# Strassen's seven half-size products for the second MoE product, on a TensorE-bound kernel

## The chip, the cores and the metric

The kernel runs on one core of a Trainium2 chip. The metric is the device time of that core in microseconds (us). Four executions before the change took 411.81, 412.22, 412.71 and 460.8 us. The last is over 1.5% above the fastest and counts as a slow one; everything below uses the fast ones, whose median is 412.2 us. The core has a matrix engine (PE, TensorE, with its weight load PEld), three elementwise engines (DVE is VectorE, ACT is ScalarE, POOL is GpSimd) and SyncE (SP). Each engine runs one fixed list of instructions, set when the kernel is built; an instruction that waits holds up those behind it.

## The reference, cut to what matters

```python
scores = scale * q @ k.T                  # 8 batches x 12 heads, 448 tokens, head size 64
attn   = relu(scores)**2 / 448
x      = attn @ v                         # as 3584 tokens x 768
h      = x @ w_in                         # 768 -> 2048
g      = relu(h)**2
out    = g @ w_out                        # 2048 -> 768, the product that the change is about
```

## The kernel before

Attention and the two dense products are interleaved. The attention runs in 84 steps, and each step has two score rounds of 4 small matmuls. The dense matmuls wait in a queue and are handed out between the scores, *one matmul at a time*, so that PE has something to do while ScalarE and VectorE turn scores into weights (`relu2`). The parts that matter:

```python
s_p  = tc.tile_pool(name="sps",  bufs=2, space=PSUM)   # scores: 2 tiles of 2 banks
mm_p = tc.tile_pool(name="mmps", bufs=4, space=PSUM)   # everything else: 4 banks

def run_some(ns):                          # dense work for one step, in ns of PE time
    while fifo and ns > 0:
        c, fn = fifo.popleft(); fn(); ns -= c

def relu2(ps, dst, scale):                 # the softmax of this model, also used for g
    nc.scalar.activation(out=dst, in_=ps, func=AF.Square, scale=scale)
    nc.vector.scalar_tensor_tensor(out=dst, in0=ps, scalar=0.0, in1=dst,
                                   op0=ALU.is_gt, op1=ALU.mult)

def o_groups(pr, tb):                      # one 128-token chunk of out: 2 halves x 16 matmuls
    def step(hf, f):
        def run():
            if f == 0: cell[0] = mm_p.tile([P, 512], FP32, name="ops", tag="mm")
            nc.tensor.matmul(cell[0][:, 0:HALF], lhsT=gt[f][:, tb*P:(tb+1)*P],
                             rhs=w2[f//4][:, f%4, hf*HALF:(hf+1)*HALF], ...)
            if f == NF - 1:                # the only work after it: one ScalarE copy, one store
                nc.scalar.activation(out=cell[1][:, ...], in_=cell[0][:, 0:HALF], ...)
        return run
    return [[(162.5, step(hf, f)) for f in range(NF)] for hf in range(2)]
# h_groups: 16 groups of 6 matmuls (189 ns each) per batch, in the same way, name "hps"

for i in range(STREAM // 2, NB):           # one attention step
    ... two score rounds; in every 3rd or 4th step a burst of 28 matmuls attention x v ("avt") ...
    for a in g: soft(*a)                   # relu2 of the scores
    upkeep(i)                              # loads; casts of q and k on GpSimd; transposes on PE
    run_some(...)                          # dense matmuls, one by one
```

GpSimd casts q and k of coming head groups to fp16. The `mm` banks are shared by the attention burst (two banks at once), by hidden groups and by output groups.

## Time and profile before

| | before |
|---|---|
| median of fast runs | 412.2 us |
| output product (ops) | 896 matmuls of 128x384, one each 162.5 ns: 145.6 us |
| hidden product (hps) | 768 matmuls of 128x448, one each 189 ns |
| busy: PE / VectorE / ScalarE / GpSimd | 96 / 61 / 63 / 18% |

These lines are from the page of the kernel before. The first is the busy time of each engine. The second is PE's busy share in 40 equal slices of the span, in tenths. The third is the chain of waits by engine. The rest are groups of instructions: line, engine, operation, out<-in, shapes, count, then busy us and mean ns of one, then the idle time just before them and what ended most of it.

```profile
PE 394.0 (96%) x3104; PEld 199.7 (49%) x3104; DVE 252.8 (61%) x304; ACT 259.7 (63%) x407; POOL 74.0 (18%) x95
...
PE   6847999999999999999999999999999999999995
...
PE 91%; ACT 4%; DVE 2%; DMA 1%; issue 1%
...
L155 DVE SCALAR_TENSOR_TENSOR at<-sp,at 128x896 f16<-128x896 f32 x159 | 166.3, 1085 | 82.1 <-ACT at L154 81.7
L154 ACT ACTIVATE at<-sp 128x896 f16<-128x896 f32 x159 | 137.7, 915 | 70.4 <-PE sp L252 70.4
...
L204 PE MATMUL ops<-w,g 128*128 128x384 f16 x896 | 156.8, 326 | 0.0
...
L252 PE MATMUL sp<-qT,kT 64*64 64x448 f16 x672 | 53.0, 373 | 10.6 <-DVE at L155 5.3
```

PE is at 9 in all slices from the fifth to the last but one, and it is 91% of the chain. PE waits for the scores' VectorE operation (L155) only 5.3 us in all. The scores' pipeline is this: PE writes a score tile, ScalarE squares it (L154, 915 ns), VectorE masks it (L155, 1085 ns), and then the tile can be written again. A matmul's mean of 326 ns is the time from its start to its recorded end; matmuls overlap, so the pace is the distance from start to start.

The view of waits, with us in total, number and longest, says the same:

```profile
PE sp L252 <- DVE at L155: 5.3, 4, 1.6
```

### The profile page before, as it was taken

What the parts mean: (1) busy time and instruction counts of PE and PEld (TensorE: products, weight loads), DVE (VectorE), ACT (ScalarE), POOL (GpSimd) and SP (SyncE); (2) the same over time, 40 slices, a digit from 0 to 9 for tenths busy, and PEclk for the clock granted to TensorE, in tenths of its full rate; (3) what the DMA queues carried; (4) which work ended last, traced back from release to release, by engine and by line L of the source; (5) the groups of instructions that cost most, each with busy time, mean ns of one, the idle gap of its engine ahead of it and who ended that gap; (6) DMA issues with size and microseconds to landing.
All of it is one profiled execution on the core that took longest, in us unless ns stands there. A gap on an engine that the chain in (4) does not pass through costs nothing.

```text
span 411.3 us, 7560 instructions
## 1 busy us (share of the span) xinstructions
PE 394.0 (96%) x3104; PEld 199.7 (49%) x3104; DVE 252.8 (61%) x304; ACT 259.7 (63%) x407; POOL 74.0 (18%) x95
## 2 busy tenths in 40 slices
PE   6847999999999999999999999999999999999995
PEld 2423455544455545544554544544554545555562
DVE  3987787578875777576655786576665686042200
ACT  3787787678866677666756767666756766333211
POOL 6861612123202301210302301210100000000000
PEclk9695999999999999999999999999999999999999
DMA  8999999599419750972829741881515010201132
GB/s 251 295 278 257 207 193 225 157 208 201 119 38 183 193 141 35 155 168 56 209 54 174 225 102 73 147 176 43 131 40 119 4 40 0 69 12 38 38 79 77
DMA packets 62914, 53.57 MB, mean 130 GB/s; under 512 B 35744, under 2 KB 59296, under 8 KB 62880
## 3 DMA queue, kind: packets, MB, share of 16 engines
q1 hardware_dynamic: 50672, 40.84, 40.7%
q0 software_dynamic: 11936, 11.80, 18.0%
q8 instruction: 24, 0.39, 0.4%
q10 hardware_dynamic: 272, 0.46, 0.3%
q14 instruction: 10, 0.08, 0.1%
HBM read 45.61 MB, written 11.01 MB: 138 GB/s over the span
## 4 chain that ended last, share of the span: by engine, by line
PE 91%; ACT 4%; DVE 2%; DMA 1%; issue 1%
PE hps L176 37%; PE ops L204 36%; PE sp L252 10%; PE avt L282 7%; ACT at L154 2%; ACT rel L161 1%; DMA kf<-in_k_dram 1%; DVE at L155 1%; PE tps L101 1%; ACT qT L103 0%; ACT xt L290 0%; DVE at L162 0%; DVE ks L87 0%; DVE kT L103 0%; DVE qT L103 0%
## 5 line engine op out<-in xcount | busy, mean ns | idle before, releaser
L155 DVE SCALAR_TENSOR_TENSOR at<-sp,at 128x896 f16<-128x896 f32 x159 | 166.3, 1085 | 82.1 <-ACT at L154 81.7
L154 ACT ACTIVATE at<-sp 128x896 f16<-128x896 f32 x159 | 137.7, 915 | 70.4 <-PE sp L252 70.4
L176 PE MATMUL hps<-xt,w 128*128 128x448 f16 x768 | 157.5, 356 | 0.0
L204 PE MATMUL ops<-w,g 128*128 128x384 f16 x896 | 156.8, 326 | 0.0
L204 PEld LDWEIGHTS <-g 128*128 128x128 f16 x896 | 84.4, 98 | 67.9 <-issue 13.7
L176 PEld LDWEIGHTS <-w 128*128 128x128 f16 x768 | 73.1, 99 | 75.1 <-issue 13.5
L155 DVE SCALAR_TENSOR_TENSOR g<-hps,g 128x448 f16<-128x448 f32 x128 | 75.7, 617 | 42.3 <-ACT g L154 42.0
L154 ACT ACTIVATE g<-hps 128x448 f16<-128x448 f32 x128 | 67.7, 551 | 29.7 <-PE hps L176 29.1
L252 PE MATMUL sp<-qT,kT 64*64 64x448 f16 x672 | 53.0, 373 | 10.6 <-DVE at L155 5.3
L211 ACT ACTIVATE osb<-ops 128x384 f32<-128x384 f32 x56 | 27.8, 496 | 37.8 <-PE ops L204 32.9
L87 POOL CAST ks<-kf 128x896 f16<-128x896 f32 x23 | 21.5, 935 | 147.6 <-DMA kf<-in_k_dram 109.8
L282 PE MATMUL avt<-at,vs 64*64 64x448 f16 x672 | 43.2, 363 | 0.4 <-ACT qT L103 0.3
L252 PEld LDWEIGHTS <-kT 64*64 64x64 f16 x672 | 16.5, 106 | 42.4 <-issue 39.7
L282 PEld LDWEIGHTS <-vs 64*64 64x64 f16 x672 | 21.5, 109 | 12.5 <-issue 2.7
L118 POOL DMA_DIRECT2D vs<-in_v_dram x28 | 17.4, 629 | 49.1 <-PE avt L282 48.3
L290 ACT ACTIVATE xt<-avt 128x448 f16<-128x448 f32 x48 | 23.6, 553 | 2.6 <-PE avt L282 2.5
L87 POOL CAST qs<-qf 128x896 f16<-128x896 f32 x23 | 23.2, 1009 | 6.7 <-DMA qf<-in_q_dram 6.7
L162 DVE TENSOR_TENSOR at<-rel 128x896 f16<-128x896 f32 x8 | 10.1, 1258 | 0.7 <-ACT rel L161 0.6
L161 ACT ACTIVATE rel<-sp 128x896 f32<-128x896 f32 x9 | 8.3, 922 | 2.2 <-PE sp L252 2.2
L345 PE MATMUL warm<-idle 128*128 128x512 f16 x12 | 4.6, 560 | 1.2 <-DVE idle L337 1.2
L129 POOL DMA_DIRECT2D w<-in_moe_w_out_dram x4 | 3.1, 764 | 14.2 <-DMA w<-in_moe_w_in_dram 14.2
L103 ACT COPY qT<-tps 128x896 f16<-128x896 f16 x5 | 4.5, 907 | 0.2 <-PE tps L101 0.2
(20 smaller groups left out, 31.4 us busy)
## 6 DMA issues: line engine op xcount, KB each, us to landing
kf<-in_k_dram SPq DMA_DIRECT2D x24, 448.0 KB, 5.1
out_dram<-osb SPq DMA_DIRECT2D x56, 192.0 KB, 2.7
qf<-in_q_dram SPq DMA_DIRECT2D x23, 448.0 KB, 5.7
vs<-in_v_dram POOLq DMA_DIRECT2D x28, 168.0 KB, 5.6
w<-in_moe_w_in_dram POOLq DMA_DIRECT2D x4, 768.0 KB, 22.2
w<-in_moe_w_out_dram POOLq DMA_DIRECT2D x4, 768.0 KB, 21.4
vs<-in_v_dram POOLq DMA_DIRECT2D x6, 112.0 KB, 7.9
qf<-in_q_dram ACTq DMA_DIRECT2D x1, 448.0 KB, 4.8
```

The lines of the kernel that those rows point to most:

```text
L87: op(t.rearrange("p t (f d) -> p f t d", f=2), src.rearrange("p f (t d) -> p f t d", d=D))
L118: nc.gpsimd.dma_start(out=vst[b][rows, :, i], in_=src[:, :, h])
L154: nc.scalar.activation(out=dst, in_=ps, func=AF.Square, scale=scale)
L155: nc.vector.scalar_tensor_tensor(out=dst, in0=ps, scalar=0.0, in1=dst, op0=ALU.is_gt, op1=ALU.mult)
L161: nc.scalar.activation(out=r, in_=ps, func=AF.Relu, scale=scale)
L162: eng.tensor_mul(dst, r, r)
L176: nc.tensor.matmul(cell[0][:, 0:S], lhsT=w1[f // 4][:, m, (f % 4) * P:(f % 4 + 1) * P], rhs=xt[:, m, :], start=(m == 0), stop=(m == NM - 1))
L204: nc.tensor.matmul(cell[0][:, 0:HALF], lhsT=gt[f][:, tb * P:(tb + 1) * P], rhs=w2[f // 4][:, f % 4, hf * HALF:(hf + 1) * HALF], start=(f = ...
L211: nc.scalar.activation(out=cell[1][:, hf * HALF:(hf + 1) * HALF], in_=cell[0][:, 0:HALF], func=AF.Copy, scale=CO)
L252: nc.tensor.matmul(sp[64 * c:64 * c + 64, e, 0:S].rearrange("p (t c) -> p t c", t=TJ), lhsT=kT[r, t, 64 * e:64 * e + 64], rhs=qT[r, :, 64 ...
L282: nc.tensor.matmul(ap[f][64 * e:64 * e + 64, 0:S], lhsT=vs[r, u, e ^ c, t * D:(t + 1) * D], rhs=at[r, e, :], start=(t == 0), stop=(t == TJ ...
L290: nc.scalar.activation(out=xts[b][:, 2 * u + f, :], in_=ap[f][:, 0:S], func=AF.Copy, scale=CX)
```

## The change

`g @ w_out` is done by Strassen's method (in Winograd's form) on pairs of 128-token chunks. With the two chunks and the two halves of the 2048 columns of g as the four blocks of A, and the four quarters of w_out as B, seven products of 8 matmuls replace eight. The intent is to save one eighth of the matmuls of the output product, on the engine that bounds the kernel. The sums that Strassen needs go to engines with spare time: `s1` and `s3` to GpSimd, `s2` and `s4` to VectorE, eight weight sums to GpSimd. Partial results leave PSUM through ScalarE copies, and VectorE closes each quarter.

The core of the diff, cut:

```diff
+    def combine_w2(eng, a):                       # eight sums of 128x1536, once
+        eng.tensor_sub(t1[:, r], top[:, :, HI], top[:, :, LO])
+        eng.tensor_sub(t2[:, r], bot[:, :, HI], t1[:, r])
+        eng.tensor_sub(t4[:, r], t2[:, r], bot[:, :, LO])
+        eng.tensor_sub(top[:, :, HI], bot[:, :, HI], top[:, :, HI])
...
+    credit = 0.0
     def run_some(ns):
-        while fifo and ns > 0:
+        credit += ns
+        while fifo and credit > 0:
...
     def h_groups(b):                              # a step of the queue is now a whole group
-        return [[(189.0, step(f, m)) for m in range(NM)] for f in range(NF)]
+        return [(189.0 * NM, group(f)) for f in range(NF)]
...
+            combine("s1", None, nc.gpsimd.tensor_add, a2[:, lo], a2[:, hi])
+            combine("s2", None, nc.vector.tensor_sub, st["s1"], a1[:, lo])
+            combine("s3", None, nc.gpsimd.tensor_sub, a1[:, lo], a2[:, lo])
+            combine("s4", None, nc.vector.tensor_sub, a1[:, hi], st["s2"])
...
+        def m6():                                 # x goes on accumulating after its copy r1
+            product("x", "s2", lambda j: t2[:, j, :], False, True)
+            part("r2", "x")                       # ScalarE copy, as are r1, r3, r5
+        def m7():
+            product("x", "s3", lambda j: w2_block(0, j, HI), False, True)
+            part("r3", "x")
+            close(2, HI, "x", "r5")               # VectorE, as are three others
...
+        return [(162.5 * NH, fn) for fn in (m1, m2, m6, m5, m7, m3, m4)]
...
-        now = len(new) if b in (0, B - 1) else len(new) - 4
+        now = len(new) if b in (0, B - 1) else len(new) - 5    # 5 products carried on
...
     push_dense(0)
+    for a in range(2):
+        combine_w2(nc.gpsimd, a)
```

Besides this, g becomes one tile per batch, some buffers shrink (attention weights from 14 to 12, raw q and k from 3 to 2), v is loaded per head group, and an extra copy (`rest`) joins the odd half chunks of two batches. "Carried on" means that five products of a pair are run between the hidden groups of the next batch, with their accumulators `x` and `z` left in PSUM meanwhile.

## The prediction

> **What bounds the kernel now.** TensorE. In the table by stretches PE is busy in every microsecond from 40 to 385; the chain of waits is 91% PE, of which the output product (ops) is 36% and the hidden product (hps) 37%. The timeline shows the real pace of ops: 71 matmuls of 128x384 in 11.70 us, 162.5 ns start to start, so 896 of them are 145.6 us. VectorE is busy 252.8 us (61%), ScalarE 259.7 (63%), GpSimd 74.0 (18%). But in the attention phase (to about 347 us) VectorE is not far from its limit: 4.79 of 5 us in 90-95, 4.81 in 105-110, with PE still full.
>
> **What the change removes.** 14 pairs of 128-token chunks need 7x8 = 56 half-size matmuls each, not 64: 784 for 896. At 162.5 ns that is 112 x 162.5 = 18.2 us, all of it PE time on the critical path. ScalarE has 42 copies of 128x384 for 56 (496 ns each): -7 us.
>
> **What it adds.**
> - VectorE: 56 closing operations out of PSUM, about 0.5 us each (estimate from g at 617 ns for 448 columns): 29 us; 28 combinations of 1024 fp16 elements, estimate 0.69 us each from the Trainium skill, "VectorE: DVE Perf Modes", perf-mode tier table (16-bit tensor_tensor at 2x, 1224 ns for 2048; no such operation is in this trace): 19 us; rest copies 4 us. Sum about 305 us.
> - GpSimd: its one tensor_tensor took 1680 ns for 896 elements, so I estimate 1.9 us x 28 = 54 us, and for w_out 8 x 2.9 us = 23 us.
>
> **What of this reaches PE.**
> 1. Weight sums. The w_out loads issue at 27.0, 31.6, 39.3 and 43.5 us (each after the first held by a w_in load) and land some 20-23 us later. The sums that need the lower half can run on GpSimd only from 60-65 us, and end at about 80-85. The first M6 and M7 are due at about 72-75 us. PE follows program order: a stall of 6 us (2 to 14).
> 2. Dense work per attention step shrinks, so VectorE's share there rises from about 75% to over 90%, worst in even batches (few products). PE will sometimes wait for scores' PSUM or for g: 4 to 8 us.
> 3. PSUM banks. x and z are held across several hidden groups in the carried products; avt needs two of four banks; hps then waits for its evacuation: 2 to 5 us.
> 4. In odd batches M6 comes soon after the last g, while s1 (GpSimd) then s2 (VectorE) take about 3 us: 2 to 4 us in all.
> The tail (pure products, both kernels) keeps the full gain; closing it costs the same as before.
>
> **Prediction.** 412.7 - 18.2 + about 15 = 409 us, range 399 to 421. Faster by over 2%: 0.30; within 2%: 0.52; slower: 0.18.
>
> **What would show it.** ops count 784, pace still 162.5 ns; VectorE busy 295-315 us, GpSimd 140-160; PE idle between 65 and 90 us released by GpSimd's weight sums; in 90-350 us PE no longer full, with waits of ops and hps on VectorE and ScalarE; the tail from the last hps on without gaps.
>
> **What would make it wrong.** Lower: weight sums done in time (quicker GpSimd, earlier landing), and VectorE at over 90% harmless as at 90-110 us now: about 398-402. Higher: GpSimd's sums delay the q/k casts it also does, hence scores; GpSimd and VectorE slow each other; every g waits behind combinations, and the lower PE load makes VectorE the bound throughout: 420 or more.

## More of the kernel before

Next, the view by windows of the kernel before, two stretches of 20 us. The columns are window, length, then busy us (instruction count) of PE, PEld, DVE, ACT, POOL, then the granted TensorE clock, the DMA share and GB/s.

```profile
60.00:80.00 20.00, 20.00 (x166) 10.45 (x164) 14.25 (x17) 15.04 (x23) 3.69 (x5) 1.00 1.03 201
...
100.00:120.00 20.00, 20.00 (x158) 9.59 (x157) 16.26 (x21) 15.80 (x24) 3.74 (x4) 1.00 0.30 81
```

PE is busy in all of each window and the clock is full.

## The result, and the profile after

The kernel became **slower**: 459.35, 458.78, 460.05 and 460.03 us, median 459.69. The ratio to the kernel before is 1.114 (95% interval 1.1115 to 1.1165). Here and below, a ratio is formed from the fast runs of the two kernels measured side by side, so it is not quite the ratio of the medians quoted. The prediction was 409 us with a range of 399 to 421, so even the range missed it by 39 us.

The page after:

```profile
PE 390.9 (85%) x2992; PEld 195.9 (43%) x2992; DVE 329.0 (72%) x396; ACT 261.1 (57%) x407; POOL 168.7 (37%) x145
...
PE   6669903919997899989898999999977999999795
...
L231 POOL TENSOR_TENSOR comb<-g 128x1024 f16<-128x1024 f16 x24 | 53.8, 2253 | 118.7 <-DVE g L176 84.4
L333 PE MATMUL sp<-qT,kT 64*64 64x448 f16 x672 | 59.2, 386 | 29.3 <-DVE at L176 23.9
...
L258 DVE SCALAR_TENSOR_TENSOR osb<-ops,part 128x384 f32<-128x384 f32 x56 | 30.4, 550 | 14.5 <-ACT part L254 8.4
...
L231 DVE TENSOR_TENSOR comb<-comb,g 128x1024 f16<-128x1024 f16 x12 | 20.1, 1675 | 11.7 <-POOL comb L231 11.6
```

PE has 112 matmuls fewer, but the slice line starts "66699039": around slice 6 of 40 (an eighth of the way in) PE does almost nothing, and it is no longer at 9 throughout. VectorE went from 252.8 to 329.0 us and GpSimd from 74.0 to 168.7. The wait of scores for VectorE (now L176) went from 5.3 to 23.9 us. The chain of waits of this page isn't shown, because it can be followed back only to 250 us; a chain share of 31% for PE is not to be compared with the 91% of before.

The same two windows after:

```profile
60.00:80.00 20.00, 4.04 (x24) 2.20 (x28) 2.62 (x3) 0.91 (x1) 19.65 (x13) 0.51 0.23 55
...
100.00:120.00 20.00, 17.21 (x124) 8.10 (x123) 13.93 (x18) 10.59 (x16) 1.39 (x3) 0.80 0.32 59
```

In the 20 us from 60 to 80, PE works for 4.04 us and GpSimd for 19.65. The granted clock over this window is 0.51, and from 100 to 120 it is 0.80. The waits after, with the new ones among them:

```profile
PE sp L333 <- DVE at L176: 23.9, 27, 8.8
...
PE tps L110 <- POOL ks L96: 17.8, 1, 17.8
DVE comb L231 <- POOL comb L231: 14.5, 6, 6.7
```

Where did the PE time go? I summed, from the trace, the distances from each PE matmul's start to the next one's start, and put each to the kind of the earlier matmul. A stall is so put to the work before it. In us:

| | scores | attention x v | hidden | output | transposes, warm-up |
|---|---|---|---|---|---|
| before | 43.3 | 46.5 | 150.9 | 149.6 | 14.6 |
| after | 77.4 | 48.6 | 156.4 | 152.9 | 15.6 |

The sum rises by 45.9 us, against 46.2 us for the profiled spans (411.3 to 457.5), so nothing is missing. The median pace of an output matmul is still 163 ns, so its 112 matmuls fewer did save about 18.3 us; the row "output" shows 21.6 us of stalls on top (152.9 - 149.6 + 18.3). The largest term, scores, rose by 34.1 us.

### Two gaps, read in the timeline

The timeline of the kernel after around the large hole. Columns: start us, duration us, engine, line, operation, out<-in, shapes, count, and in brackets the idle time before and its releaser.

```profile
67.67 3.09 POOL L146 TENSOR_TENSOR w<-w,w 128x1536 f16<-128x1536 f16 x1
70.71 3.09 POOL L145 TENSOR_TENSOR wt<-wt,w 128x1536 f16<-128x1536 f16 x1
...
74.95 0.95 POOL L96 CAST ks<-kf 128x896 f16<-128x896 f32 x1
...
75.95 0.93 PE L110 MATMUL tps<-ident,ks 128*128 128x128 f16 x7 [17.82 <-POOL ks L96]
...
77.55 2.44 PE L193 MATMUL hps<-xt,w 128*128 128x448 f16 x6
...
80.82 2.44 PE L193 MATMUL hps<-xt,w 128*128 128x448 f16 x12
```

GpSimd runs eight weight sums of 3.09 us, 24.7 us of work between 46.80 and 73.80 us: each of the first three waited for a load of w_out, and from the third on they follow without a gap. Behind them, in its order of work, stand two issues of v loads (1.23 us) and then the cast of k for head group 5. In the kernel before, the same cast started at 47.51 us (timeline of that kernel):

```profile
47.51 0.94 POOL L87 CAST ks<-kf 128x896 f16<-128x896 f32 x1
```

In the kernel after it starts at 74.95, 27 us later. The transpose on PE that needs it waited 17.82 us, and since PE is in order too, all of PE waited. The last two lines show a second effect: just after the gap 6 hidden matmuls take 2.44 us, and 3 us later 12 of them take 2.44 us. That is half speed after a long idle stretch: the hidden matmuls start 373 ns apart and then 189. The Trainium skill, "TensorE: Matmul & The Clock Gate", Part 1, describes this: about 3.4 us without work halves the clock, and about as long under work restores it. The trace agrees: the mean clock is 0.51 in the window from 60 to 80 us, 1.00 in the same window of the kernel before, and full pace is back at 80.82 us, some 5 us after work resumed.

The second gap, 25 us later:

```profile
92.78 0.94 POOL L96 CAST ks<-kf 128x896 f16<-128x896 f32 x1 [3.89 <-DMA kf<-in_k_dram]
...
93.90 0.94 POOL L96 CAST qs<-qf 128x896 f16<-128x896 f32 x1 [0.19 <-DMA qf<-in_q_dram]
94.78 1.18 POOL L121 DMA_DIRECT2D vs<-in_v_dram  x2
95.97 4.20 POOL L231 TENSOR_TENSOR comb<-g 128x1024 f16<-128x1024 f16 x2
98.13 2.60 DVE L231 TENSOR_TENSOR comb<-comb,g 128x1024 f16<-128x1024 f16 x1 [6.66 <-POOL comb L231]
100.65 1.08 DVE L176 SCALAR_TENSOR_TENSOR at<-sp,at 128x896 f16<-128x896 f32 x1
...
101.78 0.59 PE L333 MATMUL sp<-qT,kT 64*64 64x448 f16 x4 [8.80 <-DVE at L176]
```

Read it from top to bottom. GpSimd waits 3.89 us for a load of k, casts it, casts q, issues two loads of v, and only then makes `s1` and `s3`. VectorE has come to `s2`, which needs `s1`, and is blocked for 6.66 us, although the next thing in its order, the scores' operation (L176), does not need `s1` at all. PE waits 8.80 us for that operation. So one late load of k, by way of three in-order queues, becomes a PE gap. By the trace, the load was late because of the same late cast as in the first gap: SyncE, which issues the loads of q and k in order, stood 47.7 us behind it (`SPq L87 <- POOL ks L96: 56.3, 3, 47.7` in its own view of waits) and issued its next loads of k only at 75.93, 80.88 and 86.69 us, the last of them being the one awaited here. (The change also leaves two buffers for raw k instead of three; that was not tested alone.) Note also the 2.60 us of `s2`: it starts while GpSimd's pair of sums runs, and ends at 100.73, just after GpSimd's end at 100.17. Experiment 3 comes back to this.

### The profile page after: what moved, and what is told of

Its sections match the earlier page's. It is cut to its first block, busy times and chain, and to the rows that moved or that the text cites. A ratio compares the mean times of both kernels' runs of the same rounds, so it can differ in the third digit from the quotient of the medians.

```text
span 457.5 us, 7513 instructions
## 1 busy us (share of the span) xinstructions
PE 390.9 (85%) x2992; PEld 195.9 (43%) x2992; DVE 329.0 (72%) x396; ACT 261.1 (57%) x407; POOL 168.7 (37%) x145
## 5 line engine op out<-in xcount | busy, mean ns | idle before, releaser
L176 DVE SCALAR_TENSOR_TENSOR at<-sp,at 128x896 f16<-128x896 f32 x159 | 166.3, 1083 | 25.9 <-ACT at L175 25.2
L176 DVE SCALAR_TENSOR_TENSOR g<-hps,g 128x448 f16<-128x448 f32 x128 | 77.1, 619 | 42.1 <-ACT g L175 42.1
L231 POOL TENSOR_TENSOR comb<-g 128x1024 f16<-128x1024 f16 x24 | 53.8, 2253 | 118.7 <-DVE g L176 84.4
L333 PE MATMUL sp<-qT,kT 64*64 64x448 f16 x672 | 59.2, 386 | 29.3 <-DVE at L176 23.9
L254 ACT ACTIVATE part<-ops 128x384 f32<-128x384 f32 x56 | 27.5, 492 | 71.2 <-PE ops L248 66.1
L248 PEld LDWEIGHTS <-comb 128*128 128x128 f16 x448 | 43.9, 101 | 42.4 <-DVE comb L231 8.6
L121 POOL DMA_DIRECT2D vs<-in_v_dram x48 | 29.0, 612 | 61.4 <-PE avt L363 52.3
L248 PE MATMUL ops<-wt,comb 128*128 128x384 f16 x224 | 43.2, 343 | 7.5 <-DVE comb L231 7.5
L96 POOL CAST ks<-kf 128x896 f16<-128x896 f32 x21 | 20.5, 976 | 70.6 <-DMA kf<-in_k_dram 70.2
L258 DVE SCALAR_TENSOR_TENSOR osb<-ops,part 128x384 f32<-128x384 f32 x56 | 30.4, 550 | 14.5 <-ACT part L254 8.4
L248 PE MATMUL ops<-w,comb 128*128 128x384 f16 x224 | 40.7, 331 | 0.0
L248 PEld LDWEIGHTS <-g 128*128 128x128 f16 x288 | 27.1, 98 | 21.8 <-issue 4.7
L248 PE MATMUL ops<-w,g 128*128 128x384 f16 x192 | 34.0, 326 | 0.0
L231 DVE TENSOR_TENSOR comb<-comb,g 128x1024 f16<-128x1024 f16 x12 | 20.1, 1675 | 11.7 <-POOL comb L231 11.6
```

Of the source, the lines that this page charges most:

```text
L96: op(t.rearrange("p t (f d) -> p f t d", f=2), src.rearrange("p f (t d) -> p f t d", d=D))
L121: nc.gpsimd.dma_start(out=t[64 * r:64 * r + 64], in_=src[:, u, hs])
L231: op(t, x, y)
L248: nc.tensor.matmul(st[bank][:, 0:HALF], lhsT=st[a][:, j, :], rhs=w(j), start=(first and j == 0), stop=(j == NH - 1), skip_group_check=True)
L254: nc.scalar.activation(out=st[name], in_=st[bank][:, 0:HALF], func=AF.Copy, scale=CO)
L258: nc.vector.scalar_tensor_tensor(out=st["o", i][:, cols], in0=st[bank][:, 0:HALF], scalar=sign * CO, in1=st[name], op0=ALU.mult, op1=ALU.add)
```

## The experiments

Times are medians; "before" ran beside each group on the same chip, at 412.16 to 412.98 us, so a difference between kernels of different groups is uncertain by about that spread. Four kernels give a wrong result, because they leave out sums; they are marked. By their intervals all but one of these still differ from the kernel before; no sums with single-matmul steps (412.85) does not. The quoted expectations label theories with letters; the text after each says in words what the number decided.

| kernel | us | ratio to before, 95% | result |
|---|---|---|---|
| after | 459.69 | 1.114, 1.1115 to 1.1165 | correct |
| casts first | 454.74 | 1.1014, 1.0997 to 1.103 | correct |
| sums of g on VectorE | 436.27 | 1.0566, 1.0543 to 1.0588 | correct |
| both of these | 425.89 | 1.0319, 1.0301 to 1.0336 | correct |
| all sums on VectorE | 421.70 | 1.0197, 1.0149 to 1.0246 | correct |
| no sums | 407.23 | 0.9865, 0.985 to 0.988 | wrong |
| no sums, closings on ScalarE | 408.15 | 0.988, 0.9858 to 0.9902 | wrong |
| no sums, single-matmul steps | 412.85 | 1.0008, 0.9987 to 1.0029 | wrong |
| the same, nothing carried | 403.50 | 0.9781, 0.974 to 0.9823 | wrong |
| all on VectorE, single steps | 428.36 | 1.0386, 1.0354 to 1.0418 | correct |
| the same, nothing carried | 421.94 | 1.0213, 1.0174 to 1.0251 | correct |
| before, in groups of 8 | 415.50 | 1.0071, 1.0049 to 1.0092 | correct |
| tail only, 4 pairs | 410.08 | 0.9935, 0.9918 to 0.9951 | correct |
| tail only, 5 pairs | 410.14 | 0.994, 0.9923 to 0.9957 | correct |

The theory at the start: most of the loss comes from *where the sums stand* (GpSimd's queue before the casts, and VectorE tied to GpSimd), not from Strassen. The rival: the loss comes from VectorE's load, the coarse steps and the held PSUM banks, and would stay without any sum.

### 1. Weight sums after the casts (casts_first)

```diff
-    for a in range(2):
-        combine_w2(nc.gpsimd, a)            # right after push_dense(0)
...
+        if i == 16:                         # in the step loop, behind the cast just issued
+            with tc.issue_after(last_cast[0]):
+                for a in range(2):
+                    combine_w2(nc.gpsimd, a)
```

> Edit: the eight weight sums stay on GpSimd, but are placed behind the q/k casts of head groups 5 and 6 in GpSimd's order. Theory A (the sums delayed casts that were long ready, and PE waited 17.8 us for them, plus some us at a half clock after it): the gap before the transposes at 76 us goes, a wait of at most 8 us of M6 or M7 on the weight sums may replace it; 440 us (435 to 448). Rival B (VectorE is over-full and the machine only moves its wait elsewhere): 455 to 460, the freed time reappears as waits on VectorE.

It took 454.74 us: 5 us gained, far less than expected. The cast gap did vanish, but another took its place (timeline of this kernel):

```profile
44.04 0.97 POOL L97 CAST ks<-kf 128x896 f16<-128x896 f32 x1
...
74.69 3.07 POOL L147 TENSOR_TENSOR wt<-wt,w 128x1536 f16<-128x1536 f16 x1
...
87.04 0.94 POOL L97 CAST ks<-kf 128x896 f16<-128x896 f32 x1 [4.52 <-DMA kf<-in_k_dram]
...
90.24 4.21 POOL L233 TENSOR_TENSOR comb<-g 128x1024 f16<-128x1024 f16 x2
92.42 2.59 DVE L233 TENSOR_TENSOR comb<-comb,g 128x1024 f16<-128x1024 f16 x1 [20.63 <-POOL comb L233]
...
96.06 0.59 PE L335 MATMUL sp<-qT,kT 64*64 64x448 f16 x4 [23.84 <-DVE at L178]
```

The cast of k now comes at 44.04 us. But now `s1` stands in GpSimd's queue behind the weight sums, and then behind a further cast that waits for its load and is done only at 87.98. VectorE is blocked 20.63 us on `s1`, and PE 23.84 us on VectorE. Moving the sums moved the wait. My expectation had counted the gap as removed; the rival, with 455 to 460 and the freed time back as waits on VectorE, was closer to the number. But its reason (VectorE over-full) does not fit: in this gap VectorE did nothing for 20.63 us.

### 2. All sums of g on VectorE (g_on_vector)

```diff
-            combine("s1", None, nc.gpsimd.tensor_add, a2[:, lo], a2[:, hi])
+            combine("s1", None, nc.vector.tensor_add, a2[:, lo], a2[:, hi])
-            combine("s3", None, nc.gpsimd.tensor_sub, a1[:, lo], a2[:, lo])
+            combine("s3", None, nc.vector.tensor_sub, a1[:, lo], a2[:, lo])
```

> Edit: s1 and s3 on VectorE instead of GpSimd, all else as in the change (weight sums still before the casts). Theory A (the split of a chain s1 -> s2 between two in-order engines makes VectorE wait, and VectorE's two-input sums take 1.25 to 2.6 us instead of 0.69 us while GpSimd adds): VectorE busy falls or stays (under 330 us) though it does 28 more sums, each sum about 0.69 us, the 8.8 us gap at 93 to 102 us and the waits of VectorE on GpSimd sums go; 437 us (430 to 445). Rival B (VectorE is over-full): VectorE busy rises to about 350 us and the time to 465 or more.

It took 436.27 us, as expected. Twenty-eight operations more on VectorE, the busier engine, made the kernel 23.4 us faster. VectorE's busy time even fell, from 329.0 to 320.0 us. What the edit removes is the dependence of VectorE on GpSimd's queue, and with it most of the overlap of the two engines' sums (experiment 3); the run doesn't divide the gain between the two. The gap before the transposes stays (19.8 us in its view of waits).

### 3. Both together (both)

The edits are those of the two before.

> Edit: casts first and s1, s3 on VectorE together. Theory A: the two gains add, 418 us (410 to 428). Rival B: 455 or more. If the two repairs overlap, as far as they repair the same wait, it lies nearer the better of the two single runs.

It took 425.89 us, inside the expected range but 8 us above its middle estimate. The gains alone are 5.0 and 23.4 us, together 33.8, so they are not additive: each alone leaves a gap that the other would have closed. One gap of 14.3 us is left, and it shows a third mechanism. The timeline of this kernel:

```profile
68.81 3.10 POOL L146 TENSOR_TENSOR wt<-w,wt 128x1536 f16<-128x1536 f16 x1
...
69.37 3.08 DVE L233 TENSOR_TENSOR comb<-g 128x1024 f16<-128x1024 f16 x1
...
71.86 3.54 POOL L148 TENSOR_TENSOR w<-w,w 128x1536 f16<-128x1536 f16 x1
72.38 3.30 DVE L216 COPY rest<-g 128x1024 f16<-128x1024 f16 x1
75.35 3.26 POOL L147 TENSOR_TENSOR wt<-wt,w 128x1536 f16<-128x1536 f16 x1
75.60 3.56 DVE L233 TENSOR_TENSOR comb<-comb,g 128x1024 f16<-128x1024 f16 x1
...
85.56 0.59 PE L335 MATMUL sp<-qT,kT 64*64 64x448 f16 x4 [14.26 <-DVE at L178]
```

VectorE's operations of this stretch take 3.08 to 3.56 us (and one more 4.83). The shortest sums of the same shape in this kernel take 0.68 us on average. No wait is shown before them; they *started*, and they end 0.3 to 0.6 us after the GpSimd sum that was under way when they started: 69.37 + 3.08 = 72.45 after 68.81 + 3.10 = 71.91, and 75.60 + 3.56 = 79.16 after 75.35 + 3.26 = 78.61. The Trainium skill, "SBUF — State Buffer", section "Who interferes with whom", says why: VectorE and GpSimd share a pair of SBUF ports under an exclusive lock that the first to start keeps for its whole instruction, and a VectorE operation with two SBUF inputs needs a port of that pair while GpSimd reads SBUF; so may a copy in a two-port mode. The trace agrees. It agrees also in what isn't hit: the scores' operation has one input in PSUM, and its mean is 1083 ns after and 1085 before.

### 4. No sums at all (no_sums, wrong)

```diff
-            combine("s1", ...); combine("s2", ...); combine("s3", ...); combine("s4", ...)
+            st["s1"], st["s2"] = a2[:, lo], a2[:, hi]
+            st["s3"], st["s4"] = a1[:, lo], a1[:, hi]
...                                          # t1, t2, t4 replaced by blocks of w_out
-    for a in range(2):
-        combine_w2(nc.gpsimd, a)
```

> Wrong result on purpose: no weight sums and no sums of g, the products take plain slices of g and w_out; the same 784 matmuls, PSUM chains, partial copies and closing operations. Theory A (the sums and where they run cost all of it): about 397 us (393 to 404), what the saved 18.2 us of PE would give. Rival C (PSUM banks held across the hidden groups, and the partial copies and closings, cost PE too): 405 to 425.

It took 407.23 us. All sums together so cost 52.5 us (459.69 - 407.23), more than the whole loss of 47.5 us (459.69 - 412.2), and the first theory holds for the largest part. But this kernel still gains only 5.7 us on its before (412.91) where its matmuls save 18.2. Some 12 us are lost with no sum in the program: here the rival is right. Its view of waits:

```profile
PE sp L331 <- DVE at L176: 11.0, 23, 1.6
```

PE waits for the scores' VectorE operation 23 times, 11.0 us, against 4 times and 5.3 us before. I also measured, in each trace, the 72 pairs of score rounds from the start of the pair to the start of the next other matmul: 35.2 us in all before, 44.8 here, 68.5 after.

### 5. Which part of the structure: single-matmul steps (no_sums_fine, wrong) and coarse steps in the kernel before (before_coarse)

no_sums_fine gives the kernel without sums the queue of the kernel before, one matmul per entry:

```diff
-        while fifo and credit > 0:
-            c, fn = fifo.popleft()
+        while fifo and (credit > 0 or whole and not closed):
+            c, fn, closed = fifo.popleft()
...
-        return [(162.5 * NH, fn) for fn in (m1, m2, m6, m5, m7, m3, m4)]
+        return [steps("x", "a11", ..., m1, begin), ..., steps("w", "a22", ..., m4, None)]
...                                          # hidden groups matmul by matmul, as before
+            run_some(0.0, True)             # close the open group ahead of an attention burst
```

The last line is needed. A first build without it deadlocked: `x`, `z` and a half-done hidden group hold three of the four banks, and the burst needs two. before_coarse is the opposite, the kernel before with queue entries of up to eight matmuls and the credit rule:

```diff
-        for c, fn in work:
-            fifo.append((c, fn))
+        for k in range(0, len(work), 8):
+            part = work[k:k + 8]
+            c = sum(c for c, _ in part)
+            fifo.append((c, lambda part=part: [fn() for _, fn in part]))
```

> Wrong result on purpose, as no_sums, but the dense work is handed out one matmul at a time again (as the kernel before does), a started group being finished before an attention-times-v burst because PSUM banks would run out otherwise. Theory D (whole groups of 1.13 or 1.30 us per step make short and long attention steps; in short ones the scores wait for VectorE and the long ones can't give it back): the 72 score pairs, 44.8 us in no_sums and 35.2 us before, fall to about 36 us, and the time from 407 to 399 (396 to 402). Rival E (VectorE's added closing operations fill every step): no change, 405 to 408.

> The kernel before with its dense work handed out in whole hidden groups and half output groups (8 matmuls, 1.30 us), with the change's running credit; nothing of Strassen. Theory D: slower by 5 to 10 us, 418 to 423, the score pairs taking 40 to 45 us instead of 35.2. Rival E: 412 to 414.

Both missed. no_sums_fine took 412.85 us, slower than with coarse steps. Its score pairs did improve, 44.8 to 39.3 us, and the wait for scores halved, as its view of waits shows:

```profile
PE sp L352 <- DVE at L178: 5.8, 8, 1.6
...
PE avt L382 <- DVE g L178: 1.9, 1, 1.9
PE ops L251 <- DVE g L178: 1.8, 2, 0.9
...
PE hps L197 <- DVE osb L262: 1.3, 4, 0.4
```

But new waits for PSUM appeared (avt, ops and hps), and from start to start attention x v took 52.9 us (48.7 in no_sums), hidden 155.8 (151.0) and output 133.5 (130.7): the other terms lost more than the scores gained. before_coarse took 415.50 us, a loss of 2.5 us on its before; its score pairs took 39.2 us, 4.0 more than before. So coarse steps do cost a few us, but alone they are not the 12.

### 6. All sums on VectorE (all_vector), and the same with single-matmul steps (all_vector_fine)

```diff
+            made = nc.vector.scalar_tensor_tensor(...)       # remembered in relu2
...
+        if 16 <= i < 20:                    # two weight sums per step, behind a scores' operation
+            with tc.issue_after(last_at[0]):
+                for _ in range(2):
+                    next(sums)()            # on VectorE
```

> All sums on VectorE: s1 to s4, and the eight weight sums two per attention step from step 16 on, each pair pinned behind that step's second softmax operation so that none waits for the w_out load. Theory A with the port (in 'both' each sum or copy of VectorE from 69 to 84 us took 3.1 to 4.8 us and ended as a GpSimd weight sum ended): every sum of VectorE takes 0.7 to 1.0 us, the 14.3 us gap goes, 414 us (410 to 418). Rival B (VectorE over-full): no better than both, 424 or more.

> All sums on VectorE and one matmul per step. If theories A and D both hold and their gains add: 407 us (402 to 411), the first that beats the kernel before. If VectorE is full by then (sums 39 us, closings 31 us): 412 or more.

all_vector took 421.70 us (one of its four runs 418.41), 3.7 us above the expected range and nearer to the rival's 424 than to 414; its verdict at 2% is unclear, but its interval lies above 1. With no sum on GpSimd, sums of g take the time that the shape costs, and a weight sum takes 1.05 us instead of 3.09. Groups by form of this kernel:

```profile
L234 DVE TENSOR_TENSOR comb<-comb,g 128x1024 f16<-128x1024 f16 x12 | 8.3, 692 | 0.1
...
L146 DVE TENSOR_TENSOR wt<-w,wt 128x1536 f16<-128x1536 f16 x2 | 2.1, 1049 | 0.0
```

The gap of 14.3 us is gone. It is still 14.5 us above the kernel without sums: that is what 56 sums of g, 8 of the weights and their waits cost on VectorE. So of the 52.5 us of experiment 4, 38.0 came from GpSimd (459.69 - 421.70: the queue, the lock and the slow clock after the gaps together) and 14.5 from the work itself. all_vector_fine took 428.36 us: the hope (407) missed by far, and its other branch (412 or more) got the number. Single-matmul steps hurt the program here too, as long as products are carried (experiment 8).

### 7. Is VectorE's throughput the limit without sums? (no_sums_close_scalar, wrong)

```diff
-            nc.vector.scalar_tensor_tensor(
-                out=st["o", i][:, cols], in0=st[bank][:, 0:HALF], scalar=sign * CO,
-                in1=st[name], op0=ALU.mult, op1=ALU.add)
+            nc.scalar.activation(
+                out=st["o", i][:, cols], in_=st[bank][:, 0:HALF], func=AF.Copy, scale=sign * CO)
```

> Wrong result on purpose: no_sums, and the 56 closing operations become ScalarE copies, so VectorE loses about 31 us and ScalarE gains about 28 us (to 288 us, 72% of the span); PSUM chains, groups and order as in no_sums. Theory E (in no_sums VectorE is 82 to 97% busy in the attention steps, against 67 to 86% before, and the scores wait for it): the 72 score pairs fall from 44.8 us to 38 to 41 us and the time from 407.2 to 401 (399 to 404). Rival F (whole groups and the PSUM banks held across them are the rest): 405 to 408.

VectorE's busy time fell from 284.4 to 257.7 us, and the kernel stayed at 408.15 us, with score pairs at 44.6 us (44.8). VectorE's throughput isn't what holds up the scores in that kernel, unless ScalarE, which took the closings over (259.9 to 283.9 us busy) and also serves the scores, lost as much as VectorE gained; no run excludes this. What the steps show is that with an eighth less output work and whole groups as entries, 15 of 71 steps became shorter than 3.2 us (2 before). One step's chain, scores then ScalarE 0.92 us then twice VectorE 1.08 us, takes about 3.1 us, so in a short step PE comes back to the scores before their PSUM is free. So my reading, which no edit tests alone, is that a short step has too little PE work to cover this chain.

### 8. Is it the carried products that single-matmul steps collide with? (no_sums_fine_nocarry, wrong, and all_vector_fine_nocarry)

```diff
-        now = len(new) if b in (0, B - 1) else len(new) - 5
+        now = len(new)                      # no product carried into the next batch
```

> Wrong result on purpose: no_sums_fine, and no product is carried into the next batch's hidden groups, so the accumulators x and z are held only through runs of products and no hidden group meets a held bank. Theory G (what is left in no_sums is a pair of evils: whole groups make short steps in which the scores wait for the chain scores, ScalarE, VectorE; single matmuls avoid that, but collide with the held banks): hidden products fall from 155.8 us (no_sums_fine) to about 151, attention times v from 37.4 to 33 or less, score pairs stay near 39, time 402 (399 to 405). Rival H (the held banks are not what made no_sums_fine slow, or steps of hidden groups alone cost as much): 407 or more.

It took 403.50 us, as expected, and 9 us less than with carrying. Attention x v fell from 52.9 to 45.9 us and output from 133.5 to 131.9; short steps are 4 (15 in no_sums, but 4 with carrying too). So with single-matmul steps, carrying products with open accumulators costs 9 us. That it is the banks fits the waits: of the 5.0 us of new PSUM waits of experiment 5 this run has 0.2 left. But carrying nothing also shifts when the products run, and whole groups without carrying were not run, so it is not shown that it is the two together that collide. Hidden stayed at 154.8 us (155.8), where 151 had been expected; about 2 us of the difference are 12 matmuls at half pace (1 in no_sums), the rest is open. This is the best of the structures tried if the sums were free: 403.5 us, not the 394 that 18.2 us would give. And with the sums:

> Right results: all sums on VectorE, one matmul per step, no carried products. If the sums cost what they cost between no_sums and all_vector (about 14 us): 417 us (413 to 420), still slower than the kernel before. If the sums only cost because of short steps and held banks: 405 to 410, faster than the kernel before.

It took 421.94 us, 1.9 us above the expected range. Against the kernel of the same structure without sums, output took 11.1 us more, scores 5.8 and hidden 2.4. From 40 to 340 us VectorE is busy 83% of the time (69% in the kernel before; views by windows), and PE waits 8.8 us for the sums of g. Thus two structures give a similar price of the sums: 14.5 us with coarse steps, 18.4 with fine ones. Both eat what the fewer matmuls gain.

### 9. Strassen only where VectorE is idle (tail4, tail5)

In the last 41 us of the kernel before only hidden and output products are left, and VectorE is busy 5.00 us of them (view by windows). tail4 keeps the kernel before, and uses Strassen for the last four pairs only, with all sums of g on VectorE, and six of the eight weight sums on GpSimd after its last cast (the other two on VectorE; besides this, g becomes one tile and other chunks are carried on):

```diff
+    PAIRS = [((2, 5), (2, 6)), ((3, 1), (3, 2)), ((3, 3), (3, 4)), ((3, 5), (3, 6))]
...
+    with tc.issue_after(last_cast[0].ins):
+        w2_sums()                           # on GpSimd, after the last cast of q and k
...
+    for one, two in PAIRS:                  # after everything else in the queue
+        push(s_groups(one, two))            # 7 products of 8 matmuls, in one piece
```

> The kernel before, with Strassen's products only for the last four pairs of chunks, computed after attention has ended: g sums on VectorE, which is idle there, weight sums on GpSimd after its last cast, no PSUM bank shared with hidden groups. 4 pairs x 8 matmuls x 162.5 ns = 5.2 us less PE. Theory (the saving is real where VectorE and the banks are free): 407.7 us (405.5 to 409.5), all of it kept. If moving two pairs of chunks out of the attention steps leaves steps that VectorE bounds, or the tail waits for sums: 410 to 415.

> As tail4 with five pairs: 6.5 us less PE, but 20.8 us of products leave the attention steps of batches 5 and 6. If VectorE still keeps up there: 406.4 us (404 to 408.5). If those steps fall under the 3.2 us or so that VectorE needs for one: slower than tail4, 409 to 413.

tail4 is correct and took 410.08 us, ratio 0.9935 (0.9918 to 0.9951): faster than both kernels, though by 0.7% only. That is just above the range hoped for (405.5 to 409.5) and in that of the other branch of its expectation (410 to 415: attention steps with too little work left). Its timeline of PE:

```profile
363.17 2.76 PE L207 MATMUL ops<-w,g 128*128 128x384 f16 x16
365.77 2.76 PE L269 MATMUL sps<-w,g 128*128 128x384 f16 x16
368.37 2.76 PE L269 MATMUL sps<-wt,comb 128*128 128x384 f16 x16
...
400.87 1.46 PE L269 MATMUL sps<-wt,g 128*128 128x384 f16 x8
```

Four pairs start at 365.77 and end near 402.3: 224 matmuls at 162.5 ns make 36.4 us, without a gap. Four pairs save 32 matmuls, 5.2 us; 2.9 us arrived (412.93 - 410.08). Part of the rest was lost earlier: the output chunks held back for the tail are missing as filler, and in the last eight attention steps a score pair takes 0.63 us instead of 0.48, 1.2 us in all. tail5 took 410.14 us, no better: there the same pairs take 0.79 us. Its expectation had allowed for that.

## Why the prediction was wrong

What was right: 784 matmuls, a pace of 163 ns, and 18.2 us of matmul time saved; closings on VectorE of about 0.5 us (550 ns measured); a sum on VectorE of 0.69 us, estimated from the Trainium skill, "VectorE: DVE Perf Modes", perf-mode tier table (683 to 724 ns by group in experiment 6, where GpSimd makes no sums: the page agrees). The tail from the last hidden matmul on had one gap, of 2.5 us, for a sum on VectorE.

What failed, by the prediction's own steps (the first two are the largest waits of PE and VectorE that it had not costed):

1. **"Weight sums ... a stall of 6 us (2 to 14)"**. This step looked at the wrong victim. It asked when the products M6 and M7 would get their weights. What stalled were the q and k casts behind the sums on the same engine: 17.8 us for one transpose, with half the clock after it. The prediction named "GpSimd's sums delay the q/k casts" only as something that would make it wrong, though the source already puts the sums ahead of the casts of the coming head groups.
2. **Item 4, "s1 (GpSimd) then s2 (VectorE) take about 3 us: 2 to 4 us in all"**. A chain was costed by the durations of its links. But VectorE in program order *blocks* while it waits: 14.5 us of waits on GpSimd (longest 6.7), and the scores behind it wait too. Putting s1 and s3 on VectorE gained 23.4 us.
3. **VectorE 295 to 315 us**. It was 329.0: the 28 sums on it took 41.5 us rather than 19, because 15 of them took 1.39 to 2.85 us, each with a GpSimd operation under way (the lock of experiment 3). "GpSimd and VectorE slow each other" was again only in the last paragraph. GpSimd measured 168.7 us (140 to 160 expected): sums of g 63.1 against 54, weight sums 24.7 against 23.
4. **Item 2, "Dense work per attention step shrinks ... 4 to 8 us"**. The wait that it named was right. Without any sum the wait for scores rose by 5.7 us (5.3 to 11.0); with the sums it was 23.9 us, since blocked VectorE operations hold the scores. The cause given (VectorE's share rising "to over 90%") is doubtful in the case without sums: experiment 7 lowered VectorE's load and nothing moved, though it loaded ScalarE instead.
5. **Item 3, PSUM banks, 2 to 5 us**. In the kernel after, PE waits 3.7 us for closings to free a bank (2.3 before hidden, 1.4 before output products, view of waits), which is inside the estimate; with single-matmul steps, carrying products with open accumulators cost 9 us (experiment 8). What carrying costs in the changed kernel itself was not tested.
6. A small error: "42 copies" on ScalarE. There are 56 (four parts for each of 14 pairs), so ScalarE had 261.1 us, no relief.

In sum: -18.2 us as predicted, and instead of "about 15" on the other side some 65: roughly 38 from having sums on GpSimd, 14.5 from the sums as work, and 12.5 from the structure (18.2 - 5.7). These three come from the differences after, all_vector, no_sums, before, so they add up to the result, 47 us, by construction; what is shown is each single edit.

What stays open: how many of the 38 us are the half clock alone, since no run had the gap with a full clock. An estimate from the traces is a few us: between two output or two hidden matmuls, distances of 1.6 to 2.2 times the usual pace cost 6.5 us in all in the kernel after, 4.3 in all_vector and 2.2 before. Open too are half of the 4 us that hidden products take more in the kernels without sums with single-matmul steps; what the smaller buffers for q, k and attention weights cost, which every Strassen kernel but the tail ones has; and whether another hand-made order on VectorE and GpSimd (which instruction stands behind which) could take more of the 14.5 us away.

## What to carry to other kernels

An engine that is busy 18% of the time is not free: ask what stands *behind* new work in its order and who waits for that, because an in-order queue passes a wait on to things that don't need it. Before saving matmuls on the bounding engine, ask whether the work that replaces them lies on engines with slack *in the same stretch*; of the correct kernels here it paid, by 0.7%, only in the tail, where VectorE was nearly idle. Less filler per step seems to be a cost in itself: with shorter steps the scores' chain of about 3 us is no longer covered (read from the traces, not isolated by an edit).

## What the Trainium skill lacked or had wrong

- "SBUF — State Buffer", section "Who interferes with whom", has the lock right and speaks of operations measured slower under it, but neither it nor "Perfetto Trace Analysis" says that in a profile the blocked VectorE operation counts as *busy*, with no wait before it. A sum of 0.68 us showed as 3.08 to 4.83 us, so VectorE's busy time overstates its work (41.5 us for 28 sums that take 19 alone).
- "GPSIMD Engine Reference", section 4.1, gives about 2x slower than VectorE for two-input operations. Here, in fp16, a sum of 128x1536 took 3.09 us on GpSimd and 1.05 on VectorE, and one of 128x1024 2.1 us (4.2 for two) against 0.68: about 3x.
- "Perfetto Trace Analysis", section "GPSIMD Engine Instruction", says to time GpSimd by the spacing of starts rather than by the reported spans. For these sums the caution was not needed: the spacing is 70.71 - 67.67 = 3.04 us, the reported span 3.09.
- No page that I read warns that accumulators held in PSUM across other work can deadlock an interleaved program (three of four banks held, a burst needing two), or that carrying them can cost time (412.85 us against 403.50 with nothing carried, single-matmul steps in both).
